# Remainder products of pooled attention: from masked whole-array matmuls to two half-array matmuls side by side, with new seeds for the order

## The chip, the core and the metric

The kernel runs on one core of one Trainium2 chip. The metric is device time in microseconds, as the median of several runs; the profiled execution is one further run. TensorE multiplies (PE, with its weight loads as PEld), VectorE is DVE, ScalarE is ACT, GpSimd is POOL, and SyncE (SP) issues the DMA transfers.

## What is computed

Attention over keys and values that are averaged in groups of eight, then a two-layer block with a rational function between its matrix products. All values are float32.

```python
B, H, S, D = 8, 8, 576, 64
pool, Sp = 8, 72
k_p = k.reshape(B, H, Sp, pool, D).mean(axis=3)
v_p = v.reshape(B, H, Sp, pool, D).mean(axis=3)
scores = (1 / sqrt(D)) * q @ k_p.transpose(0, 1, 3, 2)
scores = scores - max(scores)
attn = exp(scores)
attn = attn / (sum(attn) + 1e-9)
x = (attn @ v_p).transpose(0, 2, 1, 3).reshape(B * S, H * D)      # 4608 x 512
h = x @ w_in                                                        # 512 x 2048
P = a[0] + a[1] * h + a[2] * h**2 + a[3] * h**3
Q = 1 + |b[0]| * |h| + |b[1]| * h**2
out = (P / (Q + 1e-6)) @ w_out                                      # 2048 x 512
```

## The kernel before

**Tiling.** The 4608 tokens go in 18 blocks of 256 (`TOK`); 576 tokens belong to one batch entry, so six of the blocks are cut by the border of an entry, and `segs` returns one or two pieces for a block. The 2048 hidden columns go in eight units of 256. For a block, `attend` makes x (as a high and a low part in fp32r, `xs`), and then for each unit `mm1` makes h in a bank of the accumulator memory (tile `ph`, 24 matmuls of 256 columns), `rational` applies the function on ACT, DVE and POOL, and `mm2` adds to the two output banks (tile `po`, 12 matmuls of 512 columns). Products are made from high and low parts: high by high, low by high, high by low.

**Attention of a block.** Two heads form a pair j (four pairs, `NJ`), whose 2 x 72 = 144 pooled keys are too many for the 128 rows of the array. So 128 of them are the main part and the first 16 (`REM`) are the rest. `prep_k` pools the keys and turns them with the tensor engine (tiles `pk`, and `pl` for the last 64 rows). `prep_v` (`prep_v_early` for the first two entries, with products into the tiles `pvs` and `pvr`) pools the values, the main rows into `vs` and the remaining ones into `vrs`; `split_v` makes high and low parts of the main ones (`vm`) and one tile for the rest (`vr`). `attention` makes scores (tile `ps`: cut into two column halves of the array where an entry ends inside a tile of 128 tokens), the exponentials `e`, their sums, and turns them so that keys lie on partitions (`hi` and `lo`, the tile named `am`): by tensor-engine transposes for the first blocks (tiles `pm`, `pr`), and from block 4 on by DVE transposes in squares of 32 and DMA moves (`am<-e`).

The rest of two pairs is put on the 128 partitions as groups g (four copies) by m (which of two pairs) by r (16 keys): two of the copies carry the high and two the low part of the probabilities, against high and low parts of the values in `vr`, so that one product gives all the terms. In `vr` the rows that belong to the other pair are zero, by masks (`mrem`, `mrem_lo`) that `make_masks` builds on POOL from `bands`; `fourfold` is the matrix that copies the rest into the four groups.

`values` then makes x for a block. For each half c of the four pairs it takes one bank `pv`, and for each pair and piece it issues four products: high values by high probabilities, low by high, the rest (128 rows, 64 columns of weights), and high by low. After each half an ACT copy makes the high part of x and a DVE subtraction the low part.

**The order.** Nothing is issued in the order of the source. Every step is added to a `Plan` with an engine, an assumed cost and a due time. `solve` simulates the engines with these costs and gives each engine its queue; `shift` moves the due times of a few per cent of the first 1850 steps by up to four microseconds, once for each seed in `SHIFTS`, and so sets which of the many nearly equal orders is used. The queues of SP and POOL come from the same plan. While TensorE has no work in the head of the kernel, `issue` fills it with matmuls into a spare tile `idle`.

Of the kernel before, what the change touches and what calls it, by code (L numbers as in the profile page):

```python
# [100 lines left out]
class Plan:  # L101
# [6 lines left out]


    MOVED, SHARE, REACH = 1850, 0.03, 4.0  # L110
    SHIFTS = (600170, 650652, 293686, 721265, 222299, 972752, 932340, 238443, 467684, 409349, 642869, 707107)

    def __init__(self, nc):
        self.nc, self.ops, self.rings, self.now, self.slack = nc, [], {}, 0.0, 1.9
# [188 lines left out]
def tile_pooled_attention_then_rational_moe(  # L303
# [20 lines left out]
    P = 128  # L324
# [30 lines left out]
    def new(where, tag, shape, dtype, name):  # L355
        return plan.tile(*pools[where], shape, dtype, tag, name)
# [24 lines left out]
    identr = real([P, P], F32R, tag="identr", name="identr")  # L381
    ident = identr.bitcast(F32)
    zero = real([P, 1], F32R, tag="zero", name="zero")
    masks = new("cpool", "masks", [P, 6], F32, "masks")

    fourfold = new("work1", "vs", [P, P], F32, "fourfold")[:2 * REM]
    bands = new("cpool", "bands", [P, 4], F32, "bands")

    mlo, mhi = masks[:, 0:1], masks[:, 1:2]

    mrem_lo, mrem = ([masks[:, i + m:i + m + 1] for m in range(2)] for i in (2, 4))
    QC = 1.0 + 1e-6
    cbias = real([P, 1], F32, tag="cbias", name="cbias")

# [3 lines left out]
    def make_masks():  # L398
        def band(m, lo, hi):

            small("memset", m, 1.0 / G)
            if lo > 0:
                small("affine_select", out=m, in_=m, pattern=[[0, 1]], compare_op=ALU.is_ge,
                      fill=0.0, base=-lo, channel_multiplier=1)
            if hi < P:
                small("affine_select", out=m, in_=m, pattern=[[0, 1]], compare_op=ALU.is_ge,
                      fill=0.0, base=hi - 1, channel_multiplier=-1)

        band(mlo, 0, SP - REM)
        band(mhi, SP - REM, P)  # L410

        for m in range(2):
            for g in range(4):
                band(bands[:, g:g + 1], g * 32 + m * REM, g * 32 + (m + 1) * REM)
            small("tensor_tensor", out=mrem_lo[m], in0=bands[:, 1:2], in1=bands[:, 3:4],
                  op=ALU.add)
            small("tensor_tensor", out=mrem[m], in0=bands[:, 0:1], in1=bands[:, 2:3], op=ALU.add)
            small("tensor_tensor", out=mrem[m], in0=mrem[m], in1=mrem_lo[m], op=ALU.add)

# [34 lines left out]
    def load_weights(kind, u):  # L456
# [5 lines left out]
        else:  # L462
# [18 lines left out]
    kpT = [new("cpool", f"kpT{i}", [P, NJ, 2 * SP], F32, f"kpT{i}") for i in range(2)]  # L481
    vm = [[new("cpool", f"vm{s}{i}", [P, NJ, P], F32R, f"vm{s}{i}") for s in range(2)]
          for i in range(2)]
    vr = [new("cpool", f"vr{i}", [P, NJ, D], F32R, f"vr{i}") for i in range(2)]

    def prep_k(n):

# [50 lines left out]
    def prep_v_early(n):  # L538

        rows = v_rows(n)  # L540
        vs = bank(f"pvs{n}", [P, NJ * D]).rearrange("p (j d) -> p j d", d=D)
        vrs = bank(f"pvr{n}", [P, 2 * D]).rearrange("p (c d) -> p c d", d=D)
        st = early(n, 2).rearrange("p (j x) -> p j x", j=NJ)
        dma(1024, st, rows[:, REM:, :].rearrange("j r x -> r j x"))
        st = st.rearrange("p j (t d) -> p t j d", t=G)
        for t in range(0, G, 2):
            pe(1.667 * NJ * D * 2, [mm(vs, ident, st[:, s], s == 0, s == G - 1)
                                    for s in range(t, t + 2)], claims=(vs,))
        place = early(n, 1)
        for m in range(2):  # L550
            dma(64, place[m * REM:(m + 1) * REM, CW:2 * CW].rearrange("p (c x) -> p c x", c=2),
                rows[m::2, 0:REM, :].rearrange("c r x -> r c x"))
        st = place[:2 * REM, CW:2 * CW].rearrange("p (c t d) -> p t c d", c=2, t=G)
        pe(1.667 * 2 * D * G, [mm(vrs, fourfold, st[:, t], t == 0, t == G - 1)
                               for t in range(G)])
        split_v(n, vs, vrs, False)

    def prep_v(n):
        rows = v_rows(n)
        vs_all = new("work1", "vs", [P, (NJ + 2) * D], F32, f"vs{n}")  # L560
        vs = vs_all[:, 0:NJ * D].rearrange("p (j d) -> p j d", d=D)
        vrs = vs_all[:, NJ * D:(NJ + 2) * D].rearrange("p (c d) -> p c d", d=D)
        for c in (2, 0, 1):
            place = new("stage", "st", [P, 1024], F32, f"st_v{n}_{c}")
            st = place.rearrange("p (j x) -> p j x", j=2)
            if c < 2:
                dma(512, st, rows[2 * c:2 * c + 2, REM:, :].rearrange("j r x -> r j x"))
            else:
                for g in range(4):
                    for m in range(2):  # L570
                        p0 = g * 32 + m * REM
                        dma(64, place[p0:p0 + REM].rearrange("p (j x) -> p j x", j=2),
                            rows[m::2, 0:REM, :].rearrange("c r x -> r c x"))

            w = RW // 2
            while w > D:
                gp(2 * w).tensor_tensor(out=st[:, :, 0:w], in0=st[:, :, 0:w],
                                        in1=st[:, :, w:2 * w], op=ALU.add)
                w //= 2
            gp(2 * w).tensor_tensor(out=vs[:, 2 * c:2 * c + 2, :] if c < 2 else vrs,  # L580
                                    in0=st[:, :, 0:w], in1=st[:, :, w:2 * w], op=ALU.add)
        split_v(n, vs, vrs, True)

    def split_v(n, vs, vrs, port):
        vhi, vlo = vm[n % 2]
        for hh, msk in enumerate((mlo, mhi)):
            cols = slice(hh * D, (hh + 1) * D)
            act(NJ * D + 100).activation(vhi[:, :, cols], vs, AF.Copy, scale=msk)
            dve(NJ * D, port=port).scalar_tensor_tensor(
                out=vlo[:, :, cols], in0=vs, scalar=msk,  # L590
                in1=vhi[:, :, cols].bitcast(F32), op0=ALU.mult, op1=ALU.subtract)
        r = vr[n % 2].rearrange("p (c m) x -> p c m x", m=2)
        for m in range(2):
            dst = r[:, :, m, :]
            act(2 * D + 100).activation(dst, vrs, AF.Copy, scale=mrem_lo[m])
            dve(2 * D, port=port).scalar_tensor_tensor(
                out=dst, in0=vrs, scalar=mrem[m], in1=dst.bitcast(F32),
                op0=ALU.mult, op1=ALU.subtract)


    def segs(t0, n):
# [25 lines left out]
        return qs  # L627

    def attention(t, hi, lo, qs, es):


        sg = segs(t * P, P)
# [24 lines left out]
        for c in range(2):  # L657
# [20 lines left out]
            out=e, in0=e, in1=sm.rearrange("p (j h) -> p j h", h=2).unsqueeze(3).to_broadcast(  # L678
                [P, NJ, 2, SP]), op=ALU.mult)
        main = pairs[:, 0:NJ, REM:]  # L680
        rem = [pairs[:, 2 * c:2 * c + 2, 0:REM].unsqueeze(1).to_broadcast([P, 4, 2, REM])
               for c in range(2)]
        four = [pairs[:, NJ + c, REM:].rearrange("p (g m r) -> p g m r", g=4, m=2)
                for c in range(2)]
        if t >= 8:
            for c in range(2):
# [3 lines left out]
        else:  # L690
# [6 lines left out]
            for c in range(2):  # L697
# [1 line left out]
            pr = bank(f"pr{t}", [P, 2, P])  # L699
            pe(109 * 2, [("transpose", (pr[:, c, :], pairs[:, NJ + c, REM:], ident), {})  # L700
                         for c in range(2)])
            act(2 * P).copy(lo[:, NJ:, col], pr)
            dve(2 * P).tensor_tensor(
                out=lo[P // 2:, NJ:, col], in0=pr[P // 2:],
                in1=lo[P // 2:, NJ:, col].bitcast(F32), op=ALU.subtract)

    def values(i, hi, lo):

        xs = [new("work2", f"x{s}", [P, NJ, TOK], F32R, f"x{s}_{i}") for s in range(2)]
        for c in range(2):  # L710
            pv = bank(f"pv{i}_{c}", [P, 2, TOK])
            calls = []
            for jj in range(2):
                j = 2 * c + jj
                for r0, r1, n in segs(i * TOK, TOK):
                    vh, vl = vm[n % 2]
                    o = pv[:, jj, r0:r1]
                    terms = ((o, vh[:, j, :], hi[:, j, r0:r1]), (o, vl[:, j, :], hi[:, j, r0:r1]),
                             (pv[:D, jj, r0:r1], vr[n % 2][:, j, :], lo[:, NJ + c, r0:r1]),
                             (o, vh[:, j, :], lo[:, j, r0:r1]))  # L720
                    calls += [mm(dst, vals, probs, s == 0, s == 3)
                              for s, (dst, vals, probs) in enumerate(terms)]
            pe(118 * len(calls), calls, claims=xs)
            cs = slice(2 * c, 2 * c + 2)
            act(2 * TOK).copy(xs[0][:, cs, :], pv)
            dve(2 * TOK).tensor_tensor(
                out=xs[1][:, cs, :], in0=pv, in1=xs[0][:, cs, :].bitcast(F32),
                op=ALU.subtract)
        return xs
# [3 lines left out]
    def attend(i):  # L733
# [12 lines left out]
        if i >= 4:  # L746

            for a in range(4):
# [7 lines left out]
            act(NJ * TOK).copy(hi, whole[:, 0:NJ])  # L756
            dve(NJ * TOK, port=True).tensor_tensor(
                out=lo[:, 0:NJ], in0=whole[:, 0:NJ], in1=hi.bitcast(F32), op=ALU.subtract)
            half = slice(P // 2, P)
            act(2 * TOK).copy(lo[0:P // 2, NJ:], whole[0:P // 2, NJ:])  # L760
            own = es[half, 0:2, :, 0:P]
            both = [x[half, NJ:].rearrange("p c (m s) -> p c m s", m=2) for x in (lo, whole)]
            act(2 * TOK).copy(own.bitcast(F32R), both[1])
            dve(2 * TOK, port=True).tensor_tensor(
                out=both[0], in0=both[1], in1=own, op=ALU.subtract)
        return values(i, hi, lo)
# [130 lines left out]
    plan.now = HEAD + 6.0  # L897
    plan.add("pe", 0, [mm(plan.idle[:, 0], ident, ident, True, True)], early=0.0)
    plan.now = 0.0
    for g in range(4):  # L900
        small("tensor_copy", out=fourfold[:, g * 32:(g + 1) * 32], in_=ident[:2 * REM, :2 * REM])
    make_masks()
    xs, kept = {}, {}
    for at, (i, u) in enumerate(order):
# [62 lines left out]
```

## Time and profile before

| what | value |
|---|---|
| median of 3 runs | 943.76 us (943.32 to 945.35) |
| profiled execution | 945.64 us, span of its instructions 943.9 us |
| granted TensorE clock | 1.000 |
| matmuls and weight loads | 6152 each |
| busy time PE, PEld | 932.3 us, 845.0 us |
| busy time DVE, ACT, POOL | 786.0 us, 693.7 us, 528.0 us |
| DMA | 75.33 MB, mean 80 GB/s |

A line of a timeline has the start in microseconds, the time from the first start to the last end of a group of neighbouring instructions, the engine, the source line (L284 for all, since a helper records every step), the operation, the tiles, rows*columns of weights used and then the moving operand, and the count. Matmuls are pipelined: one lasts some 0.28 us from start to end but the next starts after about 0.12 us, so that the time a matmul costs is read from start to start.

### The profile page before, as it was taken

What the parts mean: (1) busy time and instruction counts of PE and PEld (TensorE: products, weight loads), DVE (VectorE), ACT (ScalarE), POOL (GpSimd) and SP (SyncE); (2) the same over time, 40 slices, a digit from 0 to 9 for tenths busy, and PEclk for the clock granted to TensorE, in tenths of its full rate; (3) what the DMA queues carried; (4) which work ended last, traced back from release to release, by engine and by line L of the source; (5) the groups of instructions that cost most, each with busy time, mean ns of one, the idle gap of its engine ahead of it and who ended that gap; (6) DMA issues with size and microseconds to landing.
All of it is one profiled execution on the core that took longest, in us unless ns stands there. A gap on an engine that the chain in (4) does not pass through costs nothing.

```text
span 943.9 us, 17079 instructions
## 1 busy us (share of the span) xinstructions
PE 932.3 (99%) x6152; PEld 845.0 (90%) x6152; DVE 786.0 (83%) x1336; ACT 693.7 (73%) x1124; POOL 528.0 (56%) x463
## 2 busy tenths in 40 slices
PE   8899999999999999999999999999999999999998
PEld 8888998989988899998999899998999899999996
DVE  7799988788989888887887997888898987887664
ACT  4788889868675877686776777676868595868674
POOL 4776866866446544445634574447545663544443
PEclk9999999999999999999999999999999999999999
DMA  9994201254235322122603160316222421202000
GB/s 275 313 390 160 45 29 46 67 127 87 49 81 105 86 34 47 29 56 53 138 5 75 51 140 8 54 37 139 47 36 50 97 50 28 51 1 57 1 23 23
DMA packets 185365, 75.33 MB, mean 80 GB/s; under 512 B 162624, under 2 KB 162624, under 8 KB 185280
## 3 DMA queue, kind: packets, MB, share of 16 engines
q1 hardware_dynamic: 185280, 74.23, 31.2%
q8 instruction: 49, 0.80, 0.4%
q14 instruction: 36, 0.29, 0.1%
HBM read 50.60 MB, written 12.58 MB: 67 GB/s over the span
## 4 chain that ended last, share of the span: by engine, by line
PE 87%; DMA 3%; SPq 3%; DVE 3%; POOL 1%; ACT 1%; issue 1%; POOLq 0%; ACTq 0%
PE ph L284 39%; PE po L284 39%; PE pv L284 4%; PE ps L284 4%; SPq L284 3%; DMA q<-in_q_dram 1%; DMA early<-in_v_dram 1%; DVE sm L284 1%; DMA st_v<-in_v_dram 1%; DVE t L284 1%; POOL w L284 0%; PE pvs L284 0%; ACT rp L284 0%; PE pq L284 0%; DVE mx L284 0%
## 5 line engine op out<-in xcount | busy, mean ns | idle before, releaser
L284 PEld LDWEIGHTS ph<-x,win 128*128 128x128 f32 x3264 | 472.7, 188 | 55.5 <-ACT w L284 0.8
L284 PE MATMUL ph<-x,win 128*128 128x256 f32 x3264 | 495.7, 282 | 1.4 <-DVE x L284 0.5
L284 PE MATMUL po<-wout,gh 128*128 128x512 f32 x1152 | 353.1, 397 | 0.1
L284 POOL TENSOR_TENSOR w<-w,r 128x512 f32<-128x512 f32 (+1 forms) x145 | 191.1, 1318 | 230.3 <-ACT r L284 228.1
L284 POOL TENSOR_TENSOR gl<-t,gh 128x512 fp32r<-128x512 f32 (+1 forms) x145 | 193.3, 1333 | 93.1 <-ACT gh L284 91.9
L284 PEld LDWEIGHTS po<-wout,gh 128*128 128x128 f32 x1152 | 185.7, 189 | 12.5 <-POOL wout L284 0.8
L284 PE MATMUL po<-wout,gl 128*128 128x512 f32 x576 | 181.8, 396 | 0.3 <-POOL gl L284 0.3
L284 ACT ACTIVATE rp<-w,cbias 128x512 f32<-128x512 f32 (+1 forms) x145 | 99.6, 687 | 59.8 <-POOL w L284 56.6
L284 DVE SCALAR_TENSOR_TENSOR t<-t,abn,rp 128x512 f32<-128x512 f32 (+1 forms) x145 | 107.3, 740 | 38.4 <-ACT rp L284 35.3
L284 DVE TENSOR_TENSOR t<-t,ph 128x512 f32<-128x512 f32 (+1 forms) x145 | 97.8, 675 | 48.7 <-ACT t L284 46.7
L284 ACT ACTIVATE r<-w,abn 128x512 f32<-128x512 f32 (+1 forms) x145 | 117.9, 813 | 20.8 <-POOL gl L284 11.4
L284 ACT ACTIVATE t<-ph,abn 128x512 f32<-128x512 f32 (+1 forms) x145 | 111.0, 767 | 26.3 <-PE ph L284 23.0
L284 ACT ACTIVATE w<-ph 128x512 f32<-128x512 f32 (+1 forms) x145 | 85.7, 591 | 40.8 <-PE ph L284 34.4
L284 DVE SCALAR_TENSOR_TENSOR t<-t,abn,ph 128x512 f32<-128x512 f32 (+1 forms) x145 | 107.0, 738 | 5.2 <-ACT w L284 1.3
L284 ACT CAST gh<-t 128x512 fp32r<-128x512 f32 (+1 forms) x145 | 88.3, 609 | 20.5 <-DVE t L284 16.9
L284 DVE SCALAR_TENSOR_TENSOR t<-rp,t 128x512 f32<-128x512 f32 (+1 forms) x145 | 99.4, 685 | 4.1
L284 DVE SCALAR_TENSOR_TENSOR rp<-w,rp 128x512 f32<-128x512 f32 (+1 forms) x145 | 99.0, 683 | 0.2
L284 PEld LDWEIGHTS po<-wout,gl 128*128 128x128 f32 x576 | 93.0, 189 | 6.4 <-POOL gl L284 0.5
L284 ACT ACTIVATE rp<-rp 128x512 f32<-128x512 f32 (+1 forms) x145 | 84.1, 580 | 3.6 <-DVE t L284 0.5
L284 POOL TENSOR_TENSOR e<-e,sm 128x576 f32<-128x576 f32 x36 | 41.8, 1175 | 51.2 <-DVE sm L284 38.7
L284 POOL TENSOR_TENSOR st_v<-st_v 128x512 f32<-128x512 f32 (+1 forms) x36 | 36.3, 1015 | 17.4 <-DMA st_v<-in_v_dram 10.7
L284 PE MATMUL ps<-kpT,qT 128*128 128x144 f32 (+1 forms) x320 | 45.6, 292 | 0.4 <-DVE kpT L284 0.2
(101 smaller groups left out, 855.9 us busy)
## 6 DMA issues: line engine op xcount, KB each, us to landing
am<-e SPq DMA_DIRECT2D x224, 48.0 KB, 2.1
out_dram<-ob SPq DMA_DIRECT2D x17, 512.0 KB, 3.1
rwin<-in_moe_w_in_dram SPq DMA_DIRECT2D x8, 1024.0 KB, 11.1
rwout<-in_moe_w_out_dram SPq DMA_DIRECT2D x8, 1024.0 KB, 14.1
st_k<-in_k_dram SPq DMA_DIRECT2D x12, 512.0 KB, 4.8
st_v<-in_v_dram SPq DMA_DIRECT2D x12, 512.0 KB, 4.2
q<-in_q_dram SPq DMA_DIRECT2D x144, 32.0 KB, 2.0
st_v<-in_v_dram SPq DMA_DIRECT2D x48, 64.0 KB, 2.2
```

The source lines that it names most:

```text
L284: getattr(engines[op.eng], name)(*map(value, args), **{k: value(v) for k, v in kw.items()})
```

## The change

The rest of a pair is laid out as m by g by r instead of g by m by r: the 64 rows of one pair lie together, in the lower or the upper half of the partitions. `vr` has two planes instead of four, without the masks that blanked the other pair; `values` issues the rest of two pairs (of the two halves c) as two products of 64 rows each, one behind the other, into two banks. Both banks are now taken at once, the products run over jj outside and c inside, and both evictions stand behind all products. The split of the rest's probabilities takes one scaled ACT copy and one DVE subtraction over all partitions. `make_masks` builds fewer bands, and `fourfold` is built by one copy. The seeds of the plan are others, 13 instead of 12.

```diff
-    SHIFTS = (600170, 650652, 293686, 721265, 222299, 972752, 932340, 238443, 467684, 409349, 642869, 707107)
+    SHIFTS = (888598, 66172, 799308, 945215, 583484, 318104, 392904, 513480, 374121, 653776,
+              554028, 565492, 419132)
...
-    vr = [new("cpool", f"vr{i}", [P, NJ, D], F32R, f"vr{i}") for i in range(2)]
+    vr = [new("cpool", f"vr{i}", [P, 2, D], F32R, f"vr{i}") for i in range(2)]
...
# prep_v (prep_v_early likewise)
-                        p0 = g * 32 + m * REM
+                        p0 = (4 * m + g) * REM
                         dma(64, place[p0:p0 + REM].rearrange("p (j x) -> p j x", j=2),
-                            rows[m::2, 0:REM, :].rearrange("c r x -> r c x"))
+                            rows[2 * m:2 * m + 2, 0:REM, :].rearrange("c r x -> r c x"))
...
# split_v
-        r = vr[n % 2].rearrange("p (c m) x -> p c m x", m=2)
-        for m in range(2):
-            dst = r[:, :, m, :]
-            act(2 * D + 100).activation(dst, vrs, AF.Copy, scale=mrem_lo[m])
-            dve(2 * D, port=port).scalar_tensor_tensor(
-                out=dst, in0=vrs, scalar=mrem[m], in1=dst.bitcast(F32),
-                op0=ALU.mult, op1=ALU.subtract)
+        r = vr[n % 2]
+        act(2 * D + 100).activation(r, vrs, AF.Copy, scale=mrem_lo)
+        dve(2 * D, port=port).scalar_tensor_tensor(
+            out=r, in0=vrs, scalar=1.0 / G, in1=r.bitcast(F32), op0=ALU.mult, op1=ALU.subtract)
...
# attention
-        rem = [pairs[:, 2 * c:2 * c + 2, 0:REM].unsqueeze(1).to_broadcast([P, 4, 2, REM])
+        rem = [pairs[:, c:NJ:2, 0:REM].unsqueeze(2).to_broadcast([P, 2, 4, REM])
                for c in range(2)]
-        four = [pairs[:, NJ + c, REM:].rearrange("p (g m r) -> p g m r", g=4, m=2)
+        four = [pairs[:, NJ + c, REM:].rearrange("p (m g r) -> p m g r", g=4, m=2)
...
-            act(2 * P).copy(lo[:, NJ:, col], pr)
+            act(2 * P).activation(lo[:, NJ:, col], pr, AF.Copy, scale=one_lo)
             dve(2 * P).tensor_tensor(
-                out=lo[P // 2:, NJ:, col], in0=pr[P // 2:],
-                in1=lo[P // 2:, NJ:, col].bitcast(F32), op=ALU.subtract)
+                out=lo[:, NJ:, col], in0=pr, in1=lo[:, NJ:, col].bitcast(F32), op=ALU.subtract)
...
# values
-        for c in range(2):
-            pv = bank(f"pv{i}_{c}", [P, 2, TOK])
+        pvs = [bank(f"pv{i}_{c}", [P, 2, TOK]) for c in range(2)]
+        for jj in range(2):
             calls = []
-            for jj in range(2):
-                j = 2 * c + jj
-                for r0, r1, n in segs(i * TOK, TOK):
-                    vh, vl = vm[n % 2]
-                    o = pv[:, jj, r0:r1]
-                    terms = ((o, vh[:, j, :], hi[:, j, r0:r1]), (o, vl[:, j, :], hi[:, j, r0:r1]),
-                             (pv[:D, jj, r0:r1], vr[n % 2][:, j, :], lo[:, NJ + c, r0:r1]),
-                             (o, vh[:, j, :], lo[:, j, r0:r1]))
-                    calls += [mm(dst, vals, probs, s == 0, s == 3)
-                              for s, (dst, vals, probs) in enumerate(terms)]
-            pe(118 * len(calls), calls, claims=xs)
+            sg = segs(i * TOK, TOK)
+            for r0, r1, n in sg:
+                vh, vl = vm[n % 2]
+                for s, (vals, probs) in enumerate(((vh, hi), (vl, hi), (vr[n % 2], lo), (vh, lo))):
+                    for c in range(2):
+                        j = 2 * c + jj
+                        if s == 2:
+                            half = slice(c * (P // 2), (c + 1) * (P // 2))
+                            calls.append(mm(pvs[c][:D, jj, r0:r1], vals[half, jj, :],
+                                            probs[half, NJ + jj, r0:r1], False, False))
+                        else:
+                            calls.append(mm(pvs[c][:, jj, r0:r1], vals[:, j, :],
+                                            probs[:, j, r0:r1], s == 0, s == 3))
+            pe(118 * 7 * len(sg) + 10, calls, claims=xs)
+        for c, pv in enumerate(pvs):
             cs = slice(2 * c, 2 * c + 2)
             act(2 * TOK).copy(xs[0][:, cs, :], pv)
...
# attend, blocks 4 and on
-            half = slice(P // 2, P)
-            act(2 * TOK).copy(lo[0:P // 2, NJ:], whole[0:P // 2, NJ:])
-            own = es[half, 0:2, :, 0:P]
-            both = [x[half, NJ:].rearrange("p c (m s) -> p c m s", m=2) for x in (lo, whole)]
-            act(2 * TOK).copy(own.bitcast(F32R), both[1])
+            own = es[:, 0:2, :, 0:P]
+            both = [x[:, NJ:].rearrange("p c (m s) -> p c m s", m=2) for x in (lo, whole)]
+            act(2 * TOK).activation(own.bitcast(F32R), both[1], AF.Copy, scale=one_lo)
```

More of the change, by code (lines that the diff above doesn't have):

```diff
@@ L383, in tile_pooled_attention_then_rational_moe @@
     zero = real([P, 1], F32R, tag="zero", name="zero")
-    masks = new("cpool", "masks", [P, 6], F32, "masks")
+    masks = new("cpool", "masks", [P, 4], F32, "masks")
     fourfold = new("work1", "vs", [P, P], F32, "fourfold")[:2 * REM]
@@ L389, in tile_pooled_attention_then_rational_moe @@
     mlo, mhi = masks[:, 0:1], masks[:, 1:2]
-    mrem_lo, mrem = ([masks[:, i + m:i + m + 1] for m in range(2)] for i in (2, 4))
+    one_lo, mrem_lo = masks[:, 2:3], masks[:, 3:4]
     QC = 1.0 + 1e-6
@@ L410, in make_masks @@
         band(mhi, SP - REM, P)
-        for m in range(2):
[L413 to L418, printed above, removed]
+        for g in range(4):
+            band(bands[:, g:g + 1], (2 * g + 1) * REM, (2 * g + 2) * REM)
+        for g in (0, 2):
+            small("tensor_tensor", out=bands[:, g:g + 1], in0=bands[:, g:g + 1],
+                  in1=bands[:, g + 1:g + 2], op=ALU.add)
+        small("tensor_tensor", out=mrem_lo, in0=bands[:, 0:1], in1=bands[:, 2:3], op=ALU.add)
+        for m in range(2):
+            band(bands[:, m:m + 1], (4 * m + 2) * REM, (4 * m + 4) * REM)
+        small("tensor_tensor", out=one_lo, in0=bands[:, 0:1], in1=bands[:, 1:2], op=ALU.add)
+        small("tensor_scalar", out=one_lo, in0=one_lo, scalar1=float(G), scalar2=None,
+              op0=ALU.mult)
     WS = 2.0 ** 8
@@ L570, in prep_v @@
                     for m in range(2):
-                        p0 = g * 32 + m * REM
+                        p0 = (4 * m + g) * REM
                         dma(64, place[p0:p0 + REM].rearrange("p (j x) -> p j x", j=2),
-                            rows[m::2, 0:REM, :].rearrange("c r x -> r c x"))
+                            rows[2 * m:2 * m + 2, 0:REM, :].rearrange("c r x -> r c x"))
             w = RW // 2
@@ L899, in tile_pooled_attention_then_rational_moe @@
     plan.now = 0.0
-    for g in range(4):
-        small("tensor_copy", out=fourfold[:, g * 32:(g + 1) * 32], in_=ident[:2 * REM, :2 * REM])
+    small("tensor_copy", out=fourfold.rearrange("p (m g r) -> p m g r", m=2, g=4),
+          in_=ident[:2 * REM, :2 * REM].rearrange("p (m r) -> p m r", m=2).unsqueeze(
+              2).to_broadcast([2 * REM, 2, 4, REM]))
     make_masks()
```

## The prediction

> **What bounds the kernel now.** I read the engine table, the slices and the chain of the page first, then the busy time by stretch, then TensorE's timeline around the products that change.
>
> ```profile
> PE 932.3 (99%) x6152; PEld 845.0 (90%) x6152; DVE 786.0 (83%) x1336; ACT 693.7 (73%) x1124; POOL 528.0 (56%) x463
> ...
> PEclk9999999999999999999999999999999999999999
> ...
> PE 87%; DMA 3%; SPq 3%; DVE 3%; POOL 1%; ACT 1%; issue 1%; POOLq 0%; ACTq 0%
> PE ph L284 39%; PE po L284 39%; PE pv L284 4%; PE ps L284 4%; SPq L284 3%; DMA q<-in_q_dram 1%; DMA early<-in_v_dram 1%; DVE sm L284 1%; DMA st_v<-in_v_dram 1%; DVE t L284 1%; POOL w L284 0%; PE pvs L284 0%; ACT rp L284 0%; PE pq L284 0%; DVE mx L284 0%
> ```
> ```profile
> 60.00:930.00 870.00, 867.92 (x5728) 787.04 (x5728) 734.32 (x1238) 650.88 (x1047) 484.68 (x388) 1.00 0.27 64
> ```
>
> TensorE's queue sets the time: between 60 and 930 us it is idle for 870.00 - 867.92 = 2.1 us, at the full clock. So each nanosecond between the starts of two neighbouring matmuls there goes into the total, and nothing that other engines save can show. The products changed are those of `values`, tile pv:
>
> ```profile
> L284 PE MATMUL pv<-am,vm x288: 192/278/363, 26.0 to 881.1; 128*128 128x256 f32 x72, 128*128 128x64 f32 x24, 128*128 128x192 f32 x24, 128*128 128x128 f32 x24
> L284 PE MATMUL pv<-am,vr x96: 222/266/337, 26.3 to 881.0; 128*64 128x256 f32 x48, 128*64 128x64 f32 x16, 128*64 128x192 f32 x16, 128*64 128x128 f32 x16
> ```
> ```profile
> 331.56 3.19 PE pv L284 x32
> ...
> 382.15 1.88 PE pv L284 x16
> ```
>
> (The first fence has min, median and max of one matmul, then the shapes; a matmul's duration overlaps the next, so I price by starts. The second is the chain.) Twelve blocks of 256 tokens have 16 products in 1.88 us; six, cut by the border of a batch entry, have 32 narrower ones in some 3.2 us. A quarter are the remainder's (vr): 96 single ones, which the change makes 48 pairs: 24 of 256 columns, 24 narrower. One block's timeline (start, length, group):
>
> ```profile
> 381.98 0.39 PE L284 MATMUL pv<-am,vm 128*128 128x256 f32 x2
> ...
> 383.16 0.28 PE L284 MATMUL pv<-am,vr 128*64 128x256 f32 x1
> 383.27 0.52 PE L284 MATMUL pv<-am,vm 128*128 128x256 f32 x3
> 383.63 0.28 PE L284 MATMUL pv<-am,vr 128*64 128x256 f32 x1
> 383.74 0.28 PE L284 MATMUL pv<-am,vm 128*128 128x256 f32 x1
> 383.86 0.64 PE L284 MATMUL ph<-x,win 128*128 128x256 f32 x4
> 384.34 0.62 PE L284 MATMUL po<-wout,gh 128*128 128x512 f32 x2
> 384.80 0.63 PE L284 MATMUL ph<-x,win 128*128 128x256 f32 x4
> ```
>
> From 381.98 to 383.86 is 1.88 / 16 = 0.117 us a slot, and the 64-column vr products cost the same and disturb no neighbour. The yardsticks: four ph take 0.48 us from start to start (383.86 to 384.34), two po 0.46.
>
> **The pairs: what they can save.** Two products side by side in one slot save a slot of 0.117 us for each wide pair: 24 x 0.117 = 2.8 us. For the narrow ones a vr slot is shorter:
>
> ```profile
> 235.04 0.22 PE L284 MATMUL pv<-am,vr 128*64 128x128 f32 x1
> 235.10 0.50 PE L284 MATMUL pv<-am,vm 128*128 128x128 f32 x3
> ```
>
> 0.06 to 0.07 us at 128 columns, which I let stand for 64 and 192 too: 24 x 0.07 = 1.7 us. Together 4.5 us.
>
> That halves of the array can work side by side the trace shows, for halves of the columns. `ps` is uncut in most token tiles (128*128) and cut where a batch entry ends (128*64, two halves):
>
> ```profile
> 388.07 1.14 PE L284 MATMUL ps<-kpT,qT 128*128 128x144 f32 x8
> 388.95 0.72 PE L284 MATMUL po<-wout,gh 128*128 128x512 f32 x2
> 389.51 0.63 PE L284 MATMUL ph<-x,win 128*128 128x256 f32 x4
> ```
> ```profile
> 539.04 0.63 PE L284 MATMUL po<-wout,gh 128*128 128x512 f32 x2
> 539.60 0.27 PE L284 MATMUL pl<-identr,ks 64*128 64x64 f32 x1
> 539.80 0.75 PE L284 MATMUL ph<-x,win 128*128 128x256 f32 x4
> 540.39 0.62 PE L284 MATMUL po<-wout,gh 128*128 128x512 f32 x2
> 540.94 0.71 PE L284 MATMUL ps<-kpT,qT 128*64 128x144 f32 x8
> 541.58 0.74 PE L284 MATMUL ph<-x,win 128*128 128x256 f32 x4
> 542.16 0.63 PE L284 MATMUL po<-wout,gl 128*128 128x512 f32 x2
> ```
>
> Uncut, ps x8 with po x2 takes 389.51 - 388.07 = 1.44 us; less 0.46 for po that is 0.98, or 0.122 a product, at no cost to the neighbours. Cut, the eight take 541.58 - 540.94 = 0.64 us: they must overlap, four pairs of 0.122 = 0.49 us and 0.15 beside.
>
> **The pairs: what they cost.** The same rows show the price of leaving the whole array and coming back. Around the cut ps: po x2 before it 0.55 instead of 0.46 (+0.09), the eight +0.15, ph x4 after it 541.58 to 542.16, 0.58 instead of 0.48 (+0.10): 0.34 us. Around `pl`, a single product of 64 rows, the nearest thing to the new one: po x2 before it 539.04 to 539.60, 0.56 (+0.10); pl itself 0.20; ph x4 after it 0.59 (+0.11). Its own streaming is small: 64 of 256 columns would be a quarter of the 0.117 us slot, 0.03, if a transpose streams as fast, and twice that at half the rate; I take 0.05. Price 0.10 + 0.15 + 0.11 = 0.36 us. Third case, pvr with 32 rows:
>
> ```profile
> 53.38 2.05 PE L284 MATMUL pvr<-early,fourfold 32*128 32x128 f32 x16
> 55.36 0.72 PE L284 MATMUL po<-wout,gh 128*128 128x512 f32 x2
> 55.92 0.63 PE L284 MATMUL ph<-x,win 128*128 128x256 f32 x4
> ```
>
> po x2 after it again 0.56 (+0.10), and 1.98 us for sixteen slots. All three shapes that use a part of the array pay on the way in and out, whatever stands beside them. I take 0.35 us for each pair, since each stands alone between whole-array products (vl before it, the last vh after it): the loop puts a pair into each of two steps jj and each segment, so 48 round trips.
>
> The rule for this in the Trainium skill is in TensorEngine Tiling (Array Packing), section Key Properties: changing the tiling mode, not just the tile, drains TensorE. The page gives no price; the 0.34 and 0.36 us above are the trace's.
>
> Wide pair: 0.35 + 0.117 + 0.01 (lag of the second) - 2 x 0.117 = +0.24, times 24 = +5.8 us. Narrow: 0.35 + 0.01 - 0.07 = +0.29, times 24 = +7.0 us. Sum +12.8 us.
>
> Bounds: no trace row has this product (fp32r, 64 rows by 64 columns, at rows 64 to 127). Low end, if it switches like the vr of now, not at all: 0.48 - 4.5 = -4.0 us. High end, if it switches and the two run one after the other: +12.8 + 4.5 = +17.3. I stand near the cut ps and pl, since one half has to sit in rows 64 to 127, which the whole array can't give.
>
> **Eviction and the head.** `values` now finishes both banks together: the first ACT copy of x no longer lies beside the second half of the products.
>
> ```profile
> 27.20 0.59 ACT L284 CAST x<-pv 128x512 fp32r<-128x512 f32 x1 [0.25 <-PE pv L284]
> ...
> 29.57 0.59 ACT L284 CAST x<-pv 128x512 fp32r<-128x512 f32 x1 [0.30 <-PE pv L284]
> ```
> ```profile
> 30.31 2.38 PE L284 MATMUL ph<-x,win 128*128 128x256 f32 x18
> ```
>
> In block 0 ph starts just behind the second copy; with both copies behind the products it starts one copy, 0.59 us, later: +0.6. In the other blocks the cover is ph and po of the block before, which the queue holds in plenty (383.86 on). The two banks are held some 0.9 us longer; the slow case would be TensorE short of a bank, and as its idle time is 2.1 us in all I take 0.
>
> **Everything else.** ACT loses one 64-row copy per block from block 4 on (14 x 0.62 us) and one vr copy per batch entry, DVE one vr product per entry:
>
> ```profile
> L284 ACT CAST e<-am 64x512 fp32r<-64x512 f32 x14 | 8.7, 618 | 0.3
> L284 ACT CAST am<-am 64x512 fp32r<-64x512 f32 x14 | 8.6, 617 | 6.1 <-DMA am<-e 6.1
> ```
>
> Worth 0 while TensorE is the bound. POOL has ten small instructions fewer before 9 us, and waits afterwards:
>
> ```profile
> 8.77 0.58 POOL L284 MEMSET kpT<- 128x576 f32 x1
> 16.51 1.15 POOL L284 TENSOR_TENSOR e<-e,sm 128x576 f32<-128x576 f32 x1 [7.17 <-DVE sm L284]
> ```
>
> It idles 7.17 us behind them: 0. The DMAs are as many and as large, with other rows: 0. `subtract` over 128 instead of 64 partitions keeps its 512 elements a partition: 0. The new seeds permute every queue, SP's and POOL's among them. The best they can give is the 2.1 us of idle time, and perhaps 1 us in the head; a worse order may lose as much: 0, +-2.
>
> Sum: 12.8 + 0.6 = +13.4 us. The profiled execution took 945.64 us (span 943.9), 1.9 above the median of the runs, 943.76; the sum is a difference of starts, the same for both, and I add it to the median: 957.2.
>
> **Rivals.** (1) The pair switches nothing. For it: the vr products of now use half the columns for free. Against: they sit at the first column, and pl and pvr, which use part of the rows, pay. Then -4.0 + 0.6 = -3.4: 940.4. It decides once a round trip costs less than 3.4 / 48 = 0.07 us. The Trainium skill's span model (TensorE: Matmul & The Clock Gate, section Measured speedup vs the span model) speaks for this side: packed products take one product's time and about 4 ns for each further one, with no term for switching; the cut ps agrees on the overlap, and contradicts the missing term by its 0.34 us. (2) The pair switches but the halves run one after the other, as they use the same columns: +17.3 + 0.6: 961.7. Against: cut ps overlaps. (3) Only half of the price, because the weights of a half array are loaded ahead: 48 x 0.175 = 8.4 less: 948.8. Against: pl and pvr show the whole price with one product and with sixteen.
>
> **How the numbers follow.** My forecast 0.65 (own range 951 to 960.5); (1) 0.16; (2) 0.07; (3) 0.08; seeds and savings that cancel the rest, 0.04. A measurement tells 0.2%, 1.9 us, from no change. Faster is (1), 0.16; same 0.04; slower 0.80. The range from 946 to 962 holds the forecast, (2) and (3), 0.80; it leaves out (1).
>
> **What would show it.** Right: pv's vr rows become 64*64; the 16 products take about 2.35 us, the 32 about 4.3; the vm group ahead of a pair has its last start 0.21 instead of 0.117 before the pair, the pair's two starts lie within 0.02, and the next vm follows 0.2 to 0.26 later; ACT's busy time falls by some 10 us with no effect; TensorE stays without idle time from 60 to 930. Wrong: 16 products in about 1.7 us (rival 1), the two halves 0.1 apart (rival 2), or an idle TensorE before ph behind `x` (a wait I hold for covered).

## The result, and the profile after

| | before | changed |
|---|---|---|
| median | 944.09 us (943.32 to 945.35, 4 runs) | 957.72 us (957.3 to 958.55, 4 runs) |
| ratio, 95% interval | | 1.0144 (1.0127 to 1.0162) |
| profiled execution | 945.64 us, span 943.9 | 957.3 us, span 955.4 |

The change costs 13.6 us, where 13.1 above that median was forecast (957.2). The head of the page:

```profile
PE 943.0 (99%) x6136; PEld 845.1 (88%) x6136; DVE 786.7 (82%) x1328; ACT 685.0 (72%) x1102; POOL 523.6 (55%) x453
...
PE 93%; SPq 3%; DMA 2%; ACT 1%; DVE 0%; issue 0%; POOL 0%; POOLq 0%; ACTq 0%
PE ph L285 41%; PE po L285 41%; PE pv L285 5%; PE ps L285 4%; SPq L285 3%; DMA early<-in_v_dram 2%; PE idle L277 1%; PE pvs L285 0%; DMA ob<-pd 0%; PE pk L285 0%; PE pq L285 0%; PE pvr L285 0%; ACT rp L285 0%; PE pm L285 0%; PE pl L285 0%
```

ACT is 8.7 us less busy and nothing comes of it; TensorE is busy for 10.7 us more. Between 60 and 930 us it stays without idle time (in such a line stand the stretch and its length, the busy time and count of PE, PEld, DVE, ACT and POOL, then the granted clock, the DMA share and GB/s):

```profile
60.00:930.00 870.00, 869.80 (x5675) 782.01 (x5673) 729.33 (x1219) 632.71 (x1011) 477.20 (x383) 1.00 0.26 63
```

The products, by shape, and then four lines of the chain. A step is here the row of pv products of one block; it is called wide where the block has 256 tokens of one entry, and cut where the border of an entry divides it:

```profile
L285 PE MATMUL pv<-am,vr x96: 240/314/331, 25.6 to 892.6; 64*64 64x256 f32 x48, 64*64 64x64 f32 x16, 64*64 64x192 f32 x16, 64*64 64x128 f32 x16
```
```profile
237.77 4.03 PE pv L285 x31
286.54 2.33 PE pv L285 x16
...
387.94 2.33 PE pv L285 x16
...
789.29 4.00 PE pv L285 x32
```

A wide step takes 2.33 us instead of 1.88, a cut one some 4.03 instead of 3.19 (of the 32 products of the first line the chain counts 31). The timeline of the step at 387.8:

```profile
387.30 0.64 PE L285 MATMUL ph<-x,win 128*128 128x256 f32 x4
387.78 0.64 PE L285 MATMUL pv<-am,vm 128*128 128x256 f32 x4
388.35 0.33 PE L285 MATMUL pv<-am,vr 64*64 64x256 f32 x2
388.61 0.97 PE L285 MATMUL pv<-am,vm 128*128 128x256 f32 x6
389.50 0.33 PE L285 MATMUL pv<-am,vr 64*64 64x256 f32 x2
389.76 0.51 PE L285 MATMUL pv<-am,vm 128*128 128x256 f32 x2
390.11 0.63 PE L285 MATMUL po<-wout,gh 128*128 128x512 f32 x2
```

Both products of a pair lie within 0.33 us from first start to last end, and their starts are 0.003 us apart; that they run side by side is settled below, where one such product alone holds the queue as long as the two. But four vm before a pair take 0.57 us to the next start instead of 0.47, the pair holds the queue for 0.26, and the first vm behind it takes 0.22 instead of 0.12.

By starts of matmuls the two spans (11.5 us apart) divide like this: the pv products 43.5 us before, 53.9 after, +10.4; the transposes (pm, pr, pq, pk: 9.7 us before, 15.8 after) +6.1, all of it in the head, the first 60 us; the idle fillers beside them -3.8; the rest -1.2. The last contains a thing I had not foreseen, a stretch at half clock:

```profile
320.00:333.00 13.00, 13.00 (x85) 11.79 (x84) 11.11 (x16) 11.31 (x18) 7.50 (x6) 1.00 0.01 1
333.80:337.90 4.10, 4.10 (x34) 3.48 (x33) 2.78 (x5) 2.15 (x4) 2.40 (x2) 1.00 0.00 0
338.00:341.30 3.30, 3.30 (x15) 3.12 (x15) 2.34 (x4) 2.18 (x4) 0.02 (x1) 0.50 0.00 0
341.40:360.00 18.60, 18.60 (x122) 16.85 (x122) 15.03 (x33) 11.01 (x17) 7.32 (x6) 1.00 0.25 40
```

From 333.9 to 337.8 TensorE works on a cut pv step, and right behind it the clock is halved for 3.41 us, which loses 1.7. The records show TensorE busy all the while.

### The profile page after: what moved, and what is told of

Same layout as the page of the kernel before. It is cut to its first block, busy times and chain, and to the rows that moved or that the text cites. A ratio compares the mean times of both kernels' runs of the same rounds, so it can differ in the third digit from the quotient of the medians.

```text
span 955.4 us, 16984 instructions
## 1 busy us (share of the span) xinstructions
PE 943.0 (99%) x6136; PEld 845.1 (88%) x6136; DVE 786.7 (82%) x1328; ACT 685.0 (72%) x1102; POOL 523.6 (55%) x453
## 4 chain that ended last, share of the span: by engine, by line
PE 93%; SPq 3%; DMA 2%; ACT 1%; DVE 0%; issue 0%; POOL 0%; POOLq 0%; ACTq 0%
PE ph L285 41%; PE po L285 41%; PE pv L285 5%; PE ps L285 4%; SPq L285 3%; DMA early<-in_v_dram 2%; PE idle L277 1%; PE pvs L285 0%; DMA ob<-pd 0%; PE pk L285 0%; PE pq L285 0%; PE pvr L285 0%; ACT rp L285 0%; PE pm L285 0%; PE pl L285 0%
## 5 line engine op out<-in xcount | busy, mean ns | idle before, releaser
L285 POOL TENSOR_TENSOR w<-w,r 128x512 f32<-128x512 f32 (+1 forms) x145 | 188.3, 1299 | 232.9 <-ACT r L285 230.0
L285 PEld LDWEIGHTS po<-wout,gh 128*128 128x128 f32 x1152 | 186.5, 189 | 13.1 <-issue 0.4
L285 PE MATMUL pv<-am,vm 128*128 128x256 f32 (+3 forms) x288 | 47.4, 291 | 0.2 <-ACT am L285 0.2
## 6 DMA issues: line engine op xcount, KB each, us to landing
rwout<-in_moe_w_out_dram SPq DMA_DIRECT2D x8, 1024.0 KB, 12.8
```

Of the source, the lines that this page charges most:

```text
L285: getattr(engines[op.eng], name)(*map(value, args), **{k: value(v) for k, v in kw.items()})
```

## The experiments

**The price belongs to the switch, not to the product: all pairs of a block behind one another.** In `values`, the products of both jj and both pieces run term by term, in one step, and only the first product into a bank starts its sum anew:

```diff
+        for some in ((0, 1), (2,), (3,)):
+            for jj in range(2):
+                for r0, r1, n in sg:
...
+                    for s in some:
...
-            pe(118 * 7 * len(sg) + 10, calls, claims=xs)
+        pe((118 * 7 * len(sg) + 10) * 2, calls, claims=xs)
```

> The changed kernel with all pairs of a block behind one another: 18 round trips instead of 48, the same products. Theory (the price belongs to the switch): 12 wide blocks save one trip of 0.34 us, 6 cut blocks save three of 0.29 us, 9.3 us in all, and 1.7 to 3.4 us if the stretch at half clock goes too: 944.5 to 949 us; wide pv step 2.0 us, inside a run of pairs 0.12 us from pair to pair. Rival (a half-array product is itself slow): 957.7 us as before, 0.22 to 0.26 us from pair to pair.

Measured 952.48 us (949.49 to 953.76), 5.2 us below the changed kernel. The step itself does as expected, in the timeline of this kernel:

```profile
386.40 1.11 PE L285 MATMUL pv<-am,vm 128*128 128x256 f32 x8
387.44 0.44 PE L285 MATMUL pv<-am,vr 64*64 64x256 f32 x4
387.81 0.74 PE L285 MATMUL pv<-am,vm 128*128 128x256 f32 x4
388.39 0.65 PE L285 MATMUL ph<-x,win 128*128 128x256 f32 x4
```

Two pairs together hold the queue for 0.37 us, against 0.26 for one: the second adds a slot of 0.11 and no price, and the wide step takes 388.39 - 386.40 = 1.99 us, as forecast. All pv products sum to 46.1 us, 7.8 less than changed, where 9.3 were forecast. The total lies 3.5 us above the forecast range. The steps have another order here, and this profile has two stretches at half clock in the head, at 27.7 and 41.3 us; the one run of this kernel at a mean clock of 1.0 took 949.49 us. The rival is out: from pair to pair it is one slot, not 0.22 to 0.26 us.

**One product instead of a pair, in the same loop.**

```diff
-                            half = slice(c * (P // 2), (c + 1) * (P // 2))
-                            calls.append(mm(pvs[c][:D, jj, r0:r1], vals[half, jj, :],
-                                            probs[half, NJ + jj, r0:r1], False, False))
+                            if c == 0:
+                                calls.append(mm(pvs[c][:D, jj, r0:r1], vals[:, jj, :],
+                                                probs[:, NJ + jj, r0:r1], False, False))
```

> The changed kernel with ONE product of all 128 rows in place of each pair, into the first bank; the rest's share of the second bank is left out and the first gets a wrong one. Same number of slots that the change hoped for, no switch, the same loop, evictions and seeds. Theory (switches): 13.6 us of the change turn into a gain: 940 to 942.5 us, wide pv steps 14 x 0.117 = 1.64 us, no stretch at half clock. Rival (late evictions or two banks held at once make TensorE wait): 953 us or more.

Measured 943.88 us (942.65 to 948.35, 10 runs), ratio to before 1.0000 (0.9989 to 1.0011). Taking the switches out takes 13.8 us off, all that the change costs. But it is no gain against before, and the range of 940 to 942.5 us is missed: the pv products sum to 39.3 us, 4.2 less than before, and the total is not 4 us less. Something else in the change gives 4 us back. In this profile most of it lies in the head, where TensorE is idle for 8.7 us of the first 60 instead of 5.8. There, before the first pv product and in a kernel without a single pair, the clock is also halved for one stretch:

```profile
9.00:13.00 4.00, 2.37 (x17) 1.74 (x15) 2.30 (x6) 0.34 (x1) 0.00 (x0) 1.00 1.02 379
13.10:16.40 3.30, 3.30 (x15) 3.24 (x15) 2.11 (x7) 0.22 (x1) 0.00 (x0) 0.50 1.06 315
```

**Two products apart: 96 round trips.** Inside each step, the order of terms and halves alone:

```diff
-                for s, (vals, probs) in enumerate(((vh, hi), (vl, hi), (vr[n % 2], lo), (vh, lo))):
-                    for c in range(2):
+                terms = ((vh, hi), (vl, hi), (vr[n % 2], lo), (vh, lo))
+                for s, c in ((0, 0), (0, 1), (1, 0), (2, 0), (1, 1), (3, 0), (2, 1), (3, 1)):
```

> The changed kernel, its order of steps unchanged, with the two half-array products of each pair apart: a whole-array product stands between them, so 96 round trips of single products instead of 48 of pairs; the same sums. Theory (the price belongs to the switch, and side by side is worth a slot): from the starts in the changed kernel's trace a wide step's half grows from 1.165 to 1.62 us and a narrow one's from 1.02 to 1.35, 24 x 0.455 + 24 x 0.33 = 18.9 us more: 974 to 981 us. Rival (a half-array product is slow by itself, wherever it stands): 957.7 us, within 2.

Measured 992.97 us (990.85 to 994.74), above the range. The steps are as forecast: wide ones 3.23 us against 2 x 1.62.

```profile
407.08 3.24 PE pv L285 x16
457.26 3.24 PE pv L285 x16
...
608.88 6.58 PE pv L285 x32
...
715.84 5.40 PE pv L285 x32
```

A single half-array product holds the queue for 0.26 us, as long as a pair does in the changed kernel, so that the second product of a pair adds next to nothing:

```profile
407.36 0.33 PE L285 MATMUL pv<-am,vr 64*64 64x256 f32 x1
407.62 0.50 PE L285 MATMUL pv<-am,vm 128*128 128x256 f32 x2
```

What is above the range is clock: this run's mean granted clock is 0.977.

```profile
340.00:350.00 10.00, 10.00 (x65) 9.04 (x65) 8.81 (x13) 8.62 (x14) 5.48 (x5) 1.00 0.01 2
350.00:357.00 7.00, 7.00 (x43) 5.66 (x41) 3.20 (x5) 3.85 (x7) 3.49 (x3) 0.96 0.00 0
357.00:361.00 4.00, 4.00 (x18) 3.71 (x19) 3.08 (x5) 2.10 (x4) 0.00 (x0) 0.64 0.00 0
```

Seven times the clock is halved, for one to three windows of 3.41 us, 44 us in all, which would be 22 us lost if all of it stood on the path (an estimate; 17 of the 44 lie in the head, where TensorE also waits). Each begins inside a pv step or 0.2 us behind the last start of one: two in the head, five at cut steps (the step at 608.88 is 1.2 us longer than the one at 715.84, which kept its clock). No wide step after the head has one.

**Pairs in the wide blocks alone.**

```diff
+                            if len(sg) == 2:
+                                if c:
+                                    continue
+                                half = slice(0, P)
```

> The changed kernel, its order of steps unchanged, with pairs in the twelve wide blocks alone; in the six cut blocks one product of all rows stands for each pair (the second bank's rest is left out there, the first gets a wrong one). Theory (switches, and the clock that halves behind the cut steps with their eight entries and exits in 4 us): cut steps from 4.03 to about 2.8 us, 7.4 us less, and no stretch at half clock behind a cut step, 1.7 to 3.4 us less: 947.5 to 950 us. Rival 1 (wide and cut steps bring on half clock alike, or the head does): 949.5 to 951. Rival 2 (the cut steps are slow for another reason than switching): 955 or more.

Measured 949.41 us (949.29 to 950.45), 8.3 below the changed kernel, inside the theory's range and at the edge of rival 1. Its pv products sum to 47.2 us, 6.7 less, which leaves 1.6 for the clock. The cut steps take 2.9 us (28 products), the wide ones 2.33 as before, and this profile has no half clock within the kernel's work; three of its four runs have a mean clock of 1.0.

```profile
331.96 2.90 PE pv L285 x28
383.30 2.34 PE pv L285 x16
```

**The changed kernel once more, for a second profile.**

> The changed kernel once more, for a second profile. Theory (half clock comes behind cut pv steps and in the head): one or two stretches of 3.41 us below full clock, each within 4 us behind the start of a pv step, none elsewhere; 957 to 959 us. Rival (they fall anywhere): stretches with no pv step in the 7 us before them.

One run, 959.15 us, 0.15 above the range. There are two stretches of 3.41 us: one at 26.6 us, inside the first pv step (24.7 to 28.5), where TensorE had been idle for 1.0 of the 3.4 us before; and one at 589.8, in the cut step of 586.5 to 590.8, where it had not been idle at all:

```profile
570.00:586.00 16.00, 16.00 (x106) 14.61 (x105) 13.47 (x19) 11.98 (x20) 7.99 (x6) 1.00 0.16 26
586.00:589.70 3.70, 3.70 (x31) 3.25 (x29) 3.63 (x5) 2.51 (x4) 1.30 (x2) 1.00 0.00 0
589.80:593.20 3.40, 3.40 (x16) 2.86 (x15) 1.97 (x4) 2.17 (x4) 1.55 (x1) 0.50 0.00 0
```

**The seeds, each set on the other kernel.** Only the line of `SHIFTS` is exchanged.

> The changed kernel with the twelve seeds of before, everything else as changed. Theory (the switches of TensorE between the whole array and halves cost the time, 48 round trips): 956 to 959.5 us, pv steps again 2.33 and 4.0 us. Rival (the new order costs it): 944 to 950 us. What lies between 954 and 956 would say that the order has 2 to 4 us of it.

> The kernel before with the thirteen new seeds alone. Theory (switches): 943 to 946 us, within 2 us of before. Rival (the new order costs it): 950 to 958 us.

The changed kernel with the old seeds: 959.05 us (956.02 to 960.14), as the theory has it; its two runs near full clock took 956.0 and 956.4, the three at 0.996 took 959.1 to 960.1. The kernel before with the new seeds: 952.02 us (950.14 to 954.06), ratio 1.0086 (1.0072 to 1.0100). That lies in the rival's range, though the rival fails on the changed kernel: seeds alone move the kernel before by 8 us. My bound of 2 us for the order was wrong. Four of its five runs have mean clocks of 0.996 to 0.998, in a kernel without pairs; the one at 1.0 took 950.14 us, so that most of the 8 us is not clock.

**Are the fillers the price of a bad order?** After its first steady step `issue` may still put in matmuls that add zero, where the plan sees TensorE idle; the kernel before has 10, with the new seeds 46.

```diff
-                elif sums:
+                elif False:
```

> The kernel before with the new seeds, and without the filler matmuls that stand in TensorE's queue after its first steady step (46 in that trace, 10 before). Theory (the 7.6 us of the new seeds on the old kernel are fillers that fall where TensorE is late against the plan, 36 more x 0.11 = 4 us, the rest idle time in the head and half clock): 946.5 to 948.5 us. Rival (the order itself stalls TensorE, and the fillers only fill the stalls): 951 to 953 us.

> The changed kernel, its order unchanged, without the 12 filler matmuls after the first steady step. Theory (fillers cost their slot where TensorE is late): 1.0 to 1.4 us faster, 956.3 to 956.8 us. Rival (they only fill stalls): 957.7 us, within 0.5; slower if they had kept the clock up. The profile is also a second look at where TensorE runs at half clock: behind a cut pv step if these steps cause it, elsewhere if not.

953.00 us (951.91 to 954.92) for the first and 960.06 us (958.51 to 960.29) for the second: no gain, and the changed kernel 2.3 us slower. My theory fell; the fillers stand in stalls that are there anyway. In the second one's profile the clock is halved from 42.8 us, inside a wide step of the head, and from 90.6 us, at the end of a cut step and not far behind where 12 fillers had stood (80.5 to 82.8 us); that they had kept the clock up fits, and is not shown by one profile.

**Is it the order or the loop that gives 4 us back?** One product for each pair, with the old seeds:

> The changed loop, evictions and layouts with one product of all rows for each pair (the second bank's rest left out, the first bank's wrong) and the twelve seeds of before. With the new seeds it took 943.9 us, 3.8 more than the products alone give (944.1 - 4.2 = 939.9). Theory A (that rest is the order, which is another with every edit and every set of seeds): anything from 939 to 948 us, but not 943.9 within 0.5 again. Theory B (it is the change's late evictions and two banks held at once, under any order): 943.4 to 944.4 us again.

And the kernel before, with nothing but the changed loop around its own products:

```diff
-        for c in range(2):
-            pv = bank(f"pv{i}_{c}", [P, 2, TOK])
+        pvs = [bank(f"pv{i}_{c}", [P, 2, TOK]) for c in range(2)]
+        for jj in range(2):
...
-            pe(118 * len(calls), calls, claims=xs)
+            pe(118 * len(calls), calls, claims=xs)
+        for c, pv in enumerate(pvs):
```

> The kernel before, masks, layouts and seeds as they were, with the changed loop alone: both pv banks taken at once, jj outside and c inside, and both evictions behind all sixteen (or 32) whole-array products; no pair, no switch. Theory B (late evictions and two banks held cost the 3.8 us that the kernels with one product of all rows did not gain): 946.5 to 949 us against 944. Rival (it is another part of the change, or the order by chance): 943 to 945.5 us. My forecast of that term was +0.6.

The first took 943.87 us (942.5 to 945.99), the same again, which was theory B's number. The second took 953.71 us (952.12 to 957.2), ratio 1.0105 (1.0078 to 1.0132): more than theory B gave. In its profile TensorE waits for the eviction's second half, which the kernel before does for 0.5 us in all:

```profile
PE ph L284 <- DVE x L284: 2.4, 2, 2.2
```

That is 2.4 us of 9.4, 1.9 more than before; the rest is spread over idle time, one stretch at half clock that follows this wait (35.2 us, again with no pair in the kernel) and an order that was not searched for this mixture. In this kernel the late evictions cost more than my 0.6 us; in the changed kernel TensorE waits for no x at all. How much of the 4 us is theirs and how much the order's stays open.

**The same price elsewhere: the single product of 64 rows made whole, in the kernel before.** `prep_k` loads and turns the last 128 rows of the pooled keys instead of the last 64, with the plan's costs unchanged, so that the order stays:

```diff
-        for c0, c1, np in ((0, 2, P), (2, 4, P), (4, 5, H * SP - 4 * P)):
+        for c0, c1, np in ((0, 2, P), (2, 4, P), (4, 5, P)):
...
-                rows[c0 * P:c0 * P + nc_ * np].rearrange("(c p) x -> p c x", c=nc_))
+                rows[min(c0 * P, H * SP - nc_ * np):min(c0 * P + nc_ * np, H * SP)].rearrange(
+                    "(c p) x -> p c x", c=nc_))
```

> The kernel before, its order of steps unchanged, with the eight transposes of 64 rows (tile pl) made whole: the last 128 rows of the pooled keys are loaded and turned instead of the last 64, so that TensorE does not leave the whole array there. Theory (switches cost everywhere on the path, not in the pairs alone): 8 round trips of 0.36 us less 0.05 more for streaming, six or seven of them on the path: 1.9 to 2.5 us faster, 941.9 to 942.6 us against 944.4. Rival (the price belongs to the new products): no difference, or slower by the 128 KB more that each of the eight loads moves.

Measured 943.39 us (942.16 to 944.74, 12 runs) against 944.01, ratio 0.9991 (0.9983 to 1.0000): less than forecast. The place itself, before and then with the whole product:

```profile
441.57 0.63 PE L284 MATMUL ph<-x,win 128*128 128x256 f32 x4
442.14 0.27 PE L284 MATMUL pl<-identr,ks 64*128 64x64 f32 x1
442.34 0.73 PE L284 MATMUL po<-wout,gl 128*128 128x512 f32 x2
442.90 0.62 PE L284 MATMUL ph<-x,win 128*128 128x256 f32 x4
```
```profile
440.37 0.63 PE L284 MATMUL ph<-x,win 128*128 128x256 f32 x4
440.83 0.27 PE L284 MATMUL pl<-identr,ks 128*128 128x128 f32 x1
440.86 0.70 PE L284 MATMUL po<-wout,gl 128*128 128x512 f32 x2
441.40 0.62 PE L284 MATMUL ph<-x,win 128*128 128x256 f32 x4
```

From the first line to the last 1.33 us against 1.03: 0.30 us for the round trip, with 64 columns more. That holds, within 0.02, at four of the seven places after the first; at the other three 0.12 to 0.19 us are saved (1.6 us over the seven). The rival is out at the place itself; the total has lost 0 to 1.6 us by its interval. Its median is the lowest of the kernels here, by little, and the interval of its ratio reaches 1.0000.

## Why the prediction was right, and where its sum was not

**What bounds the kernel, and the pair's mechanism: right.** TensorE stays without idle time (869.80 of 870.00 us between 60 and 930), the saving on ACT was worth nothing, pairs run side by side and pay on the way in and out. The last vm ahead of a pair starts 0.21 us before it, and the next comes 0.26 us behind, as forecast. Wide steps were forecast at 2.35 us and take 2.33; the pv term in all is +10.4 us where +12.8 stood.

**The narrow pairs were priced too high.** I took the same 0.35 us for them. Their round trip is cheaper, in the cut step at 237.6 us of the changed kernel:

```profile
237.61 0.56 PE L285 MATMUL pv<-am,vm 128*128 128x128 f32 x4
238.09 0.27 PE L285 MATMUL pv<-am,vr 64*64 64x128 f32 x2
238.30 0.89 PE L285 MATMUL pv<-am,vm 128*128 128x128 f32 x6
239.11 0.28 PE L285 MATMUL pv<-am,vr 64*64 64x128 f32 x2
```

The pair holds the queue for 0.21 us instead of 0.26, but that is the shorter streaming, for which I had already put 0.07 instead of 0.117. What is cheaper is the delay of the whole-array products beside the pair. Six vm between two pairs take 0.81 us here, and 0.67 between two products of all rows in the kernel with one product for a pair:

```profile
238.14 0.83 PE L285 MATMUL pv<-am,vm 128*128 128x128 f32 x6
238.81 0.22 PE L285 MATMUL pv<-am,vr 128*64 128x128 f32 x1
```

That is 0.14 us more; in the wide steps of the same two kernels it is 0.89 against 0.71, 0.18 more. So the 32 products of a cut step take 4.03 us and not 4.3, and it grows by (4.03 - 3.19) / 4 = 0.21 us a pair, not 0.29: 24 x 0.08 = 1.9 us less. A wide pair costs 0.225, not 0.24.

**The clock: a term that was missing.** I read 1.00 in every slice before and carried it over. The changed kernel's runs have mean clocks of 0.998 and 0.996, one or two stretches of 3.41 us at half clock, 1.7 us each if TensorE is on the path; the runs of the kernel before that were timed beside the experiments stayed at 0.999 or more, but for one at 0.998. So about 2.5 us of the 13.6 come from here (an estimate, the mean of the four runs), and they stand in for what the narrow pairs did not cost. With the old seeds the changed kernel has two runs near full clock, and they took 956.0 and 956.4 us.

The stretches are of two kinds. At cut steps after the head, TensorE has not been idle in the 6.8 us before one, and the profiles show a dose: with one product for a pair, or with all pairs of a block in one round trip, no cut step has a stretch; with four trips, three of 24 have one (four profiles, one of them with none); with eight, five of six. In the head, where four profiles of kernels with pairs have stretches, they also come without any pair: at 13.1 us in the kernel with one product for a pair, at 35.2 us with the late evictions alone, at 25.6 us in the kernel before with new seeds and no fillers. In the 3.4 us before each of these stretches in the head TensorE had been idle for 0.8 to 2.4 us; but the kernel before has a gap of 1.5 us there, at 24.1 us, and no stretch behind it, so idle time alone is not shown to be the cause.

In the Trainium skill, TensorE: Matmul & The Clock Gate (Part 1, What's actually happening) gives a window of 3413 ns over which the activity of TensorE is watched, which is the length found here. Its section HAM oscillation asks that no idle gap be longer than some 3.4 us. That does not cover this case, as no gap between matmuls in these profiles is longer than 2.5 us. What the monitor counts is not shown.

**The seeds: wrong as a bound, harmless here.** "0, +-2" is refuted by 8 us on the kernel before. My bound came from TensorE's idle time, which caps only what a better order can gain; what a worse one can lose, stalls in the head and around 203 us, no row of before caps. On the changed kernel the two sets differ by 1.3 us, within what its runs spread by the clock.

**The late evictions: +0.6 was too little or the order took the rest.** By the two kernels with one product for a pair, everything in the change beside the switches costs about 4 us against its pure products. In the changed kernel itself only 13.6 - 10.4 - 2.5 = 0.7 us are left for it, so the parts do not simply add; the sum of starts has it as transposes that wait (+6.1 us, less 3.8 of fillers), and none of these waits is for x. That the late evictions cost anything there is not shown.

So 957.2 came out beside 957.7 as 10.4 + about 2.5 of clock + 0.7 left over, not as 12.8 + 0.6. The mechanism carries the size of the change; that it came out within 0.5 us is luck, as the clock that I left out and the narrow pairs that I priced too high cancel.

**The rivals.** No switch price (940.4): refuted by every timeline above. One after the other (961.7): refuted, as a pair holds the queue for 0.26 us and a single half-array product for 0.26 as well, and a second pair adds 0.11. Half the price (948.8): refuted, a wide pair pays 0.225 - 0.01 + 0.117 = 0.33 us. The weights of the first vm behind a pair are not loaded ahead of it: their load starts with it, at 388.61.

```profile
388.61 0.76 PEld L285 LDWEIGHTS pv<-am,vm 128*128 128x128 f32 x6
```

## What to carry to other kernels

Before packing small products into parts of the array, count the round trips: here each cost about 0.33 us around 256-column products, as much as three of them, and a pair saved one. Put all packed products together or leave the whole array alone; with one trip a block the pairs still lost (46.1 us of pv products against 43.5 before). A schedule found by search can belong to the kernel it was searched for: the new seeds cost the kernel before 8 us, while the old ones cost the changed kernel nothing clear of its spread.

## What was not expected of the hardware

The granted clock fell to one half, in units of 3.41 us, at steps in which TensorE never stopped: at five of six cut steps with eight round trips in 5.4 us, at three of 24 with four round trips in 4 us (four profiles), and at none of whole-array products alone. In the head it fell without pairs too, where TensorE had been idle for parts of the window before; no gap was longer than 2.5 us. Not expected either: the whole-array products between two narrow pairs lose less (0.14 us for six) than those between two wide ones (0.18).
